# First DFT step of the filter in 64x64 tiles: leaving out the zero blocks of a block-diagonal factor

## The chip, the core and the metric

The kernel runs on one core of a Trainium2 chip. A core has a matrix engine (TensorE, PE in the profile; its weight loads stand apart as PEld), a vector engine (DVE), a scalar engine (ACT), a general engine (POOL) and a queue engine (SP) that here issues nearly all transfers. Sixteen DMA engines move the data. The metric is the device time of one execution in microseconds; runs are told by their median.

## The reference

An adaptive layer norm block with two branches, on 2048 tokens of 640 channels, all float32:

```
mod = silu(c) @ w_mod                        # six rows of 640: sa, ca, ga, sb, cb, gb
h   = layernorm(q) * (1 + ca) + sa
k_shift = causal depthwise conv of k, 4 taps
kv  = k_shift * v
y   = irfft(rfft(kv, 4096) * rfft(ssm_k, 4096))[:2048] + kv * ssm_D    # per channel
x   = q + ga * (h * y)
h   = layernorm(x) * (1 + cb) + sb
out = x + gb * (W2 gelu(W1 h + b1) + b2)     # mixer MLP across the 2048 tokens, F = 1728
```

The change touches the long convolution alone: the transform of `ssm_k` (one filter of length 2048 for each of the 640 channels).

## The kernel before

The 640 channels go through the convolution in five blocks of 128 (`c` = 0 to 4). The convolution is a transform of length 4096 with half of the input zero, written as matrix products on the matrix engine. A channel's 2048 values are a 64 by 32 array, and the transform has two steps with small DFT matrices: `step1` over the 64-long index, `f2` over the 32-long one, with the twiddle factors in the second matrix. Two inputs go through both steps: `kv`, called side 0, and the filter `ssm_k`, called side 1. After `f2` the two spectra are multiplied (`mul` on DVE, `add` mostly on POOL, both recorded at line 60 by a helper), and `i2` and `i1` turn the product back. `gate` multiplies the result into the normed `q` and adds it to the rows.

The partition axis of a `step1` operand is 2 x 64: two halves `h` of the 128 channels, each with the 64-long index. The DFT factor `F1` (128 rows) is therefore block-diagonal: for the real and for the imaginary part (`ri`) it has 128 columns, 64 for each half, and rows of one half are zero in the columns of the other. For a step `t` (four in each block), `step1(side, t)` takes 8 pieces `a`, and multiplies each with both parts: 16 products with 128 rows contracted, 64 stationary columns and 128 moving columns (line 229). `ri` decides which half of the output partitions is written. One ACT copy (line 231) then brings the result from PSUM into the tile `Z`, whose last axis pairs two channels. `f2(g)` reads `Z` at line 245 as moving operand: 64 columns, made of 32 pairs that lie 256 elements apart. All these operands are float32; in the profile one such product shows as two weight loads and two matmuls. `i1` at line 293 works in 64x64 tiles already: 64 rows contracted, 64 columns out, four positions of the array used in turn, and the two row halves write to different PSUM banks.

The order on every engine is written out by hand, with three PSUM slots of two banks used in turn. Ahead of the loop stand the four steps of side 0 and the four steps of side 1 for block 0. In the loop over `c`, `f2` runs eight times, then `i2`, then `i1(0)`, `i1(1)` and the gates. Side 1 of the next block comes at the end: for `c` = 1, 2, 3 `step1(1, 0)` stands between `i1(0)` and `i1(1)` (line 657) and the other three behind `i1(1)` (line 665); for `c` = 0 all four stand behind `i1(1)`. The DVE order there is: gate of half 0, three operations that prepare `kv` two blocks ahead (`dv`), gate of half 1, further `kv` operations, then `mul` of `f2(0)`. In the last block these are row statistics instead. The rest of the program, from about 300 us on, is the MLP (lines 443, 974 and 1051).

## Time and profile before

| | |
|---|---|
| median of 3 runs | 712.46 us (706.91 to 717.07) |
| span of the profiled execution | 705.8 us |
| time of PE, busy | 644.5 us |
| time of DVE, busy | 492.5 us |
| time of ACT, busy | 307.1 us |
| time of POOL, busy | 155.9 us |
| matmuls of line 229 on side 1 | 640, busy 39.6 us |
| matmuls of line 229 on side 0 | 640, busy 44.3 us |
| matmuls of line 245 (`f2`) | 2560, busy 95.8 us |

The profile's span is that of the recorded instructions. The profiled execution's own time isn't given beside it; the fastest run stands 1.1 us above the span, the median 6.7 us. A matmul's duration in the profile holds its way through the array, in which several matmuls are under way at once; how fast they follow each other is read from a stretch and its count. In a timeline a row is start, length, engine, line, operation, output and inputs, and the number of instructions merged in it; a bracket at its end gives the idle time before it and what ended that. "issue" there means that nothing the profile shows was waited for. Side 1 of `step1` is named `pst<-v,p`, side 0 `pst<-v,x`.

### The profile page before, as it was taken

The page shows a single profiled execution, that of the slowest core. Times are in us where ns is not written, and L with a number is a line of the kernel's source. Part 1 is how long each engine was busy: PE and PEld are TensorE (multiplying, and loading weights), DVE is VectorE, ACT ScalarE, POOL GpSimd, SP SyncE. Part 2 cuts the span into 40 slices and gives each one's busy share as a digit, 9 for nine tenths or more (in the row PEclk, how much of TensorE's full clock was granted, in tenths as well). Part 3 has the DMA queues.
Part 4 walks back from the last instruction along what each step waited for, and adds up shares of the span by engine and source line. Part 5 has one row for each costly group of instructions (what it writes and reads, how often), then busy time and mean ns, then how long its engine had stood idle before and what let it go on. Part 6 is the DMA issues. An engine that isn't in the chain of part 4 may idle for free.

```text
span 705.8 us, 20785 instructions
## 1 busy us (share of the span) xinstructions
PE 644.5 (91%) x9131; PEld 624.2 (88%) x9131; DVE 492.5 (70%) x861; ACT 307.1 (44%) x473; POOL 155.9 (22%) x135
## 2 busy tenths in 40 slices
PE   0699779989999989977899999999999999999997
PEld 0699469889999989777899999999999999999997
DVE  7778468969879638888884312311298979888886
ACT  0664554645745645556767223222334322333331
POOL 5297039615526428100010000000000000000000
PEclk9999979999999999999999999999999999999999
DMA  9968978446333522361303543354163243555511
GB/s 180 219 205 238 350 148 168 110 76 144 68 62 88 172 59 68 115 150 30 60 1 60 99 82 60 61 103 77 52 194 105 88 149 99 166 170 170 148 60 38
DMA packets 166672, 82.80 MB, mean 117 GB/s; under 512 B 89235, under 2 KB 157622, under 8 KB 166582
## 3 DMA queue, kind: packets, MB, share of 16 engines
q1 hardware_dynamic: 162034, 80.17, 46.0%
q10 hardware_dynamic: 4548, 1.31, 1.1%
q8 instruction: 71, 1.16, 0.7%
q14 instruction: 19, 0.16, 0.1%
HBM read 70.97 MB, written 10.49 MB: 115 GB/s over the span
## 4 chain that ended last, share of the span: by engine, by line
PE 65%; DVE 16%; ACT 4%; DMA 4%; POOL 4%; issue 3%; SPq 2%; ACTq 0%; DVEq 0%; POOLq 0%
PE pst L443 21%; PE pst L974 17%; PE pst L1051 7%; PE pst L229 7%; PE pst L245 6%; PE pst L274 4%; POOL y L60 3%; DVE tap L60 3%; PE pst L293 2%; DVE kt L60 2%; DVE p L60 2%; DMA aux<-in_w_mod_dram 2%; SPq L163 2%; DVE aux L60 1%; DVE y L60 1%
## 5 line engine op out<-in xcount | busy, mean ns | idle before, releaser
L245 PEld LDWEIGHTS pst<-z,w 128*64 128x64 f32 x2560 | 94.6, 141 | 7.9 <-ACT z L231 7.3
L245 PE MATMUL pst<-z,w 128*64 128x64 f32 x2560 | 95.8, 240 | 6.2 <-ACT z L231 6.1
L60 POOL TENSOR_TENSOR y<-p 128x256 f32<-128x256 f32 x72 | 92.3, 1341 | 22.4 <-DVE p L60 21.9
L60 DVE TENSOR_TENSOR p<-pst,kt 128x512 f32<-128x512 f32 x80 | 52.4, 691 | 23.8 <-ACT kt L249 15.5
L229 PE MATMUL pst<-v,x 128*64 128x128 f32 x640 | 44.3, 297 | 23.6 <-DVE x L60 23.6
L231 ACT ACTIVATE z<-pst 128x1024 f32<-128x1024 f32 x40 | 45.9, 1148 | 42.7 <-PE pst L229 23.1
L229 PEld LDWEIGHTS pst<-v,x 128*64 128x64 f32 x640 | 42.5, 220 | 24.1 <-POOL t L468 23.5
L847 ACT ACTIVATE pst<-pst,sm 128x640 f32<-128x640 f32 x14 | 10.7, 767 | 85.7 <-PE pst L443 85.7
L249 ACT ACTIVATE kt<-pst 128x512 f32<-128x512 f32 x40 | 25.1, 627 | 47.4 <-PE pst L245 26.6
L274 PEld LDWEIGHTS pst<-v,y 32*128 32x128 f32 x1280 | 38.1, 187 | 6.7 <-POOL y L60 3.8
L229 PE MATMUL pst<-v,p 128*64 128x128 f32 x640 | 39.6, 282 | 4.2 <-issue 2.2
L274 PE MATMUL pst<-v,y 32*128 32x64 f32 x1280 | 40.0, 272 | 3.8 <-DVE y L60 2.7
L974 PE MATMUL pst<-r_z,m_w 128*128 128x320 f32 x222 | 41.6, 309 | 0.7 <-DVE m_w L60 0.7
L229 PEld LDWEIGHTS pst<-v,p 128*64 128x64 f32 x640 | 36.9, 142 | 5.6 <-issue 2.9
L962 ACT ACTIVATE m_w<-m_v 128x896 fp32r<-128x896 f32 x24 | 22.2, 949 | 38.5 <-DVE m_v L60 23.1
L60 DVE TENSOR_TENSOR tap<-tap,kt 128x512 f32<-128x512 f32 x51 | 35.6, 698 | 1.3
L60 DVE TENSOR_TENSOR kt<-in,tap 128x512 f32<-128x512 f32 x51 | 35.0, 686 | 1.5
L974 PEld LDWEIGHTS pst<-r_z,m_w 128*128 128x128 f32 x222 | 34.8, 188 | 0.9 <-DVE m_w L60 0.9
L60 DVE TENSOR_TENSOR m_w<-m_v,m_w 128x896 fp32r<-128x896 f32 x24 | 26.0, 1088 | 9.5 <-ACT m_w L962 9.5
L282 ACT ACTIVATE z<-pst 128x512 f32<-128x512 f32 x38 | 21.5, 670 | 23.2 <-PE pst L274 23.2
L962 ACT ACTIVATE m_w<-m_p 128x896 fp32r<-128x896 f32 x12 | 11.5, 954 | 41.2 <-DVE m_p L60 24.4
L443 PE MATMUL pst<-r_z,wb0b 128*128 128x320 f32 x180 | 28.1, 310 | 0.9 <-DVE u_x L60 0.9
(278 smaller groups left out, 1436.9 us busy)
## 6 DMA issues: line engine op xcount, KB each, us to landing
x<-in_B_w_dram SPq DMA_DIRECT2D x22, 512.0 KB
m_v<-in_B_w_dram SPq DMA_DIRECT2D x15, 384.0 KB
x<-in_B_w_dram SPq DMA_DIRECT2D x14, 384.0 KB
aux<-in_A_ssm_k_dram SPq DMA_DIRECT2D x10, 512.0 KB
in<-in_A_k_dram SPq DMA_DIRECT2D x36, 128.0 KB
in<-in_A_v_dram SPq DMA_DIRECT2D x36, 128.0 KB
m_x<-xs SPq DMA_DIRECT2D x28, 160.0 KB
out_dram<-m_x SPq DMA_DIRECT2D x28, 160.0 KB
```

The source lines that it names most:

```text
L60: TT = lambda eng, o, a, b, op: eng.tensor_tensor(o, a, b, op=op)
L163: sync.dma_start(KSR[64 * h:64 * h + 64].rearrange("p (i n) -> p i n", i=64), dram(ssm_k, (DC * c + 64 * h) * S, [[32, 64], [S, 64], [1, 3 ...
L229: pe.matmul(ps[64 * ri:64 * ri + 64, o:o + 128], lhs, F1[:, 128 * ri:128 * ri + 128], start=True, stop=True)
L231: evac = lambda: act.activation(Z[:, side, t].rearrange("p a k e -> p e a k"), ps.rearrange("p (e a k) -> p e a k", a=8, e=2), AF.Copy)
L245: pe.matmul(ps[64 * h:64 * h + 64, o:o + 64], W2[k1 // 32][:, 2 * (k1 % 32) + ri], rhs, start=True, stop=True)
L249: act.activation(kt.rearrange("p (m i) -> p m i", i=32), pv[:, :, 1], AF.Copy)
L274: pe.matmul(pp[qd // 2][:, o:o + 64], Y[p, ri, i:i + 2].rearrange("p i k -> p (i k)"), V2[p, 64 * ri:64 * ri + 64], start=ri == 0, stop=ri ...
L282: act.activation(o, i, AF.Copy)
L443: pe.matmul(ps[0:m, h, 0:320], w_.bitcast(F32R), r_[:, 320 * h:320 * h + 320].bitcast(F32R), start=first and i == 0, stop=last and i == 2)
L962: act.activation(W[n][0].bitcast(F32R), A[p, w_], AF.Copy)
L974: pe.matmul(bank[n], w[:, i].bitcast(F32R), r.bitcast(F32R), start=i == 0 and k == 0, stop=i == 6 and k == 2)
L1051: pe.matmul(acc[s][:, h, 0:320], w[:, f_].bitcast(F32R), u[r + h].bitcast(F32R), start=f_ == 0 and k == 0, stop=f_ == NF - 1 and k == 2)
```

## The change

On side 1 each of the 16 products of a step becomes two: half `h` contracts its own 64 rows with its own 64 columns of `F1`, in a 64x64 tile, and writes to the PSUM bank of `h`. The blocks of zeros are not multiplied any more. A step has 32 products in place of 16, each with half the rows and half the moving columns. Side 0 keeps its 16 products, but puts their 128 output columns into two runs of 64, since the order of the pieces in PSUM and in `Z` is new for both sides: the half is the outer index, the piece the inner one. The ACT copy of side 1 reads PSUM with the pairing stride of 64 elements. `f2` reads its 32 pairs as eight groups, 1024 elements apart, of four pairs, 128 elements apart. The number of waits and of semaphore signals is the same on every engine.

```diff
         for a in range(8):
             i = 8 * t + a
             lhs = KSP[:, i] if side else X.rearrange("p (m i) -> p i m", i=32)[:, i]
-            o = 512 * (a % 2) + 128 * (a // 2)
             for ri in range(2):
-                pe.matmul(ps[64 * ri:64 * ri + 64, o:o + 128], lhs, F1[:, 128 * ri:128 * ri + 128], start=True,
-                          stop=True)
+                if not side:
+                    o = ps.rearrange("p (e h i k) -> p e i h k", e=2, h=2, i=4)[64 * ri:64 * ri + 64, a % 2, a // 2]
+                    pe.matmul(o, lhs, F1[:, 128 * ri:128 * ri + 128], start=True, stop=True)
+                    continue
+                for h in range(2):
+                    r, o = slice(64 * h, 64 * h + 64), 512 * h + 64 * a
+                    pe.matmul(ps[64 * ri:64 * ri + 64, o:o + 64], lhs[r], F1[r, 128 * ri + 64 * h:128 * ri + 64 * h + 64],
+                              start=True, stop=True)
         evac = lambda: act.activation(Z[:, side, t].rearrange("p a k e -> p e a k"),
-                                      ps.rearrange("p (e a k) -> p e a k", a=8, e=2), AF.Copy)
+                                      ps.rearrange("p (a e k) -> p e a k" if side else "p (e a k) -> p e a k", a=8, e=2),
+                                      AF.Copy)
         return evac if later else evac()
...
-                    rhs = bass.AP(tensor=T_z.tensor, offset=T_z.offset + 128 * h + 2 * k1,
-                                  ap=[T_z.ap[0], [256, 32], [1, 2]])
+                    rhs = bass.AP(tensor=T_z.tensor, offset=T_z.offset + 512 * h + 2 * k1,
+                                  ap=[T_z.ap[0], [1024, 8], [128, 4], [1, 2]])
```

## The prediction

> **What bounds the kernel now.** I read the page first: the span, the busy shares, the chain by line, and the groups of the operations that the change touches.

> ```profile
> span 705.8 us, 20785 instructions
> PE 644.5 (91%) x9131; PEld 624.2 (88%) x9131; DVE 492.5 (70%) x861; ACT 307.1 (44%) x473; POOL 155.9 (22%) x135
> ...
> q8 instruction: 71, 1.16, 0.7%
> ...
> L245 PE MATMUL pst<-z,w 128*64 128x64 f32 x2560 | 95.8, 240 | 6.2 <-ACT z L231 6.1
> ...
> L229 PE MATMUL pst<-v,p 128*64 128x128 f32 x640 | 39.6, 282 | 4.2 <-issue 2.2
> ```

> PE is busy 91% of the span, but an average: the question is what ends last where side 1 of `step1` stands. Two things count later. The 640 matmuls of side 1 occupy 39.6 us, which bounds the whole matter. And queue q8, which brings instructions, carried 71 packets of 1.16 MB / 71 = 16.3 KB, while PE has 9131 loads and as many matmuls: 18262 / 71 = 257, so about one packet for 256 PE instructions.

> Next the timeline of PE around side 1, for the turn from block 1 to 2 (`c` = 1), and behind it the chain that leaves there.

> ```profile
> 148.03 2.10 PE L293 MATMUL pst<-z,v 64*64 64x64 f32 x128
> 150.06 0.66 PE L229 MATMUL pst<-v,p 128*64 128x128 f32 x8
> 151.70 1.53 PE L229 MATMUL pst<-v,p 128*64 128x128 f32 x24 [0.98 <-issue]
> 153.16 1.75 PE L293 MATMUL pst<-z,v 64*64 64x64 f32 x104
> 155.70 0.58 PE L293 MATMUL pst<-z,v 64*64 64x64 f32 x24 [0.80 <-issue]
> 156.21 5.46 PE L229 MATMUL pst<-v,p 128*64 128x128 f32 x96
> ```

> ```profile
> 156.35 1.23 DVE aux L60
> ...
> 166.82 1.28 DVE p L60 x2
> ...
> 173.57 10.61 POOL y L60 x8
> ...
> 187.37 0.66 PE pst L274 x14
> ```

> The reader should see two things. First, the chain leaves PE when `i1(1)` ends at 156.3: the gate on DVE (156.35), thirteen `kv` operations, `mul` (166.82), POOL's additions, `i2` (187.37). The 5.46 us of `step1` behind 156.21 are not in it. Second, PE stops twice, for 0.98 and 0.80 us, with nothing to wait for, and between the two resumptions lie 24 + 104 = 128 matmuls with 128 loads: exactly 256 instructions. So PE waits for its own instructions. From one resumption to the next it took 155.70 - 151.70 = 4.00 us; while `i1` needs only 2.10 us for such a block (16.4 ns for a load with its matmul, "a pair" below) and side 1 now needs 5.46 / 96 = 56.9 ns a pair.

> The other turns, in the same two views:

> ```profile
> 202.01 1.96 PE L229 MATMUL pst<-v,p 128*64 128x128 f32 x30 [0.25 <-issue]
> ...
> 251.99 0.33 PE L293 MATMUL pst<-z,v 64*64 64x64 f32 x4 [0.70 <-issue]
> 252.25 1.97 PE L229 MATMUL pst<-v,p 128*64 128x128 f32 x32
> 254.15 2.37 PE L293 MATMUL pst<-z,v 64*64 64x64 f32 x128
> 256.44 5.46 PE L229 MATMUL pst<-v,p 128*64 128x128 f32 x96
> 263.13 3.11 PE L245 MATMUL pst<-z,w 128*64 128x64 f32 x78 [1.23 <-ACT z L231]
> ```

> ```profile
> 205.74 0.72 PE pst L293 x30
> ...
> 206.49 1.22 DVE aux L60
> ```

> For `c` = 2 the block takes 205.74 - 202.01 = 3.73 us, and the gate leaves PE in the same way. I take 3.87, the middle of 3.73 and 4.00, where the trace of before has no resumption of its own. Only for `c` = 3 does side 1 itself stand on the path: `f2` starts at 263.13, when the copy behind its last step is done.

> **The change part by part.** *Side 1.* A step has 32 pairs now (32 products of two) and 64 afterwards. The new product has the shape of line 293 (64x64, 64 columns, four tile positions), so I take 16.4 ns a pair: 64 x 16.4 = 1.05 us in place of 1.82. Over 20 steps that frees 15.4 us of PE. Each step also issues 64 instructions more. Four steps make 256, one whole block: so outside of these stretches every block boundary stays at the place in the work where it is now, and inside I can move them by counting.

> *c = 1.* Until 151.70 nothing differs. Then 56 pairs of the step remain (0.92 us, to 152.6) in place of 24; `i1(1)` starts, but the next boundary comes after 128 pairs, so 72 of its pairs run (1.18 us, to 153.8) and PE stands until 155.70, as it does now. Behind that boundary 56 pairs of `i1(1)` are left in place of 24. Its end moves by 32 x 16.4 = **+0.52 us**. The gate, thirteen DVE operations and `mul` are queued behind it, POOL behind them. Further on: 72 pairs of `step1`, a stand until 155.70 + 3.87 = 159.57, 120 pairs, to 161.5 or so, where the steps now end at 161.67. So `f2` gains 0.1 at most, then meets a boundary eight pairs in (163.4, 0.3 us); `mul` has to come at 167.34 by DVE, and this is covered.

> *c = 2.* The same with 205.74: **+0.52 us**.

> *c = 3.* `i1(0)` ends as now. The step takes 1.05 us (to 253.1), 60 pairs of `i1(1)` to 254.1, a stand until 251.99 + 3.87 = 255.86 (today the boundary lies at its pair 92, hence 2.37 in place of 2.10 us), 68 pairs to 257.0, 60 pairs of `step1` to 258.0, a stand until 259.73, and 132 pairs: 261.9, the end of before. With 3.73 it would be 261.6, with 4.00 262.2: **+0.15** for the path, from -0.3 to +0.4.

> *c = 0* and the start:

> ```profile
> 35.25 2.43 ACT L231 ACTIVATE z<-pst 128x1024 f32<-128x1024 f32 x2
> ...
> 40.02 1.09 ACT L231 ACTIVATE z<-pst 128x1024 f32<-128x1024 f32 x1 [0.59 <-PE pst L229]
> 40.84 11.65 SPq L512 DMA_DIRECT2D xa<-in_A_q_dram  x16
> 52.53 12.10 SPq L512 DMA_DIRECT2D xb<-in_A_q_dram  x16
> 64.67 1.12 SPq L346 DMA_DIRECT2D v<-in_w_mod_dram  x2
> 65.83 2.94 SPq L346 DMA_DIRECT2D aux<-in_w_mod_dram  x2
> ...
> 77.27 1.28 PE L353 MATMUL tap<-aux,sm 128*32 128x320 f32 x12 [1.15 <-DMA aux<-in_w_mod_dram]
> ...
> 99.52 4.23 POOL L60 TENSOR_TENSOR t<-in,t 128x512 f32<-128x512 f32 x2 [19.27 <-DMA in<-in_A_k_dram]
> ...
> 104.00 5.38 PE L229 MATMUL pst<-v,p 128*64 128x128 f32 x64 [1.96 <-DVE aux L60]
> ...
> 116.83 5.55 POOL L60 TENSOR_TENSOR y<-p 128x256 f32<-128x256 f32 x4
> ...
> 123.01 12.45 POOL L60 TENSOR_TENSOR y<-p 128x256 f32<-128x256 f32 x10
> ```

> At the start ACT follows with four copies of 1.2 us, two of them until 37.68; so `f2` may begin at about 40.1, some 1.0 us earlier. That gain is lost at 77.27, where PE waits for a transfer: SP has been issuing without a gap since 40.84, and no transfer there waits for `f2`. For `c` = 0 the third step waits for DVE until 104.00 either way; `f2` gains 1 to 3 us, but POOL works without a gap from 99.52 to 135.46, and its additions end that stage. Both count nothing. Without these covers they would bring 1 and up to 3.

> *The new operands.* Side 0's output in two runs, side 1's copy with another stride, and `f2`'s operand in groups of four pairs have no row of their own. For `f2` one bound is 2 x 16.4 = 32.8 ns a pair (half as many tiles as `i1`) against 95.8 / 2560 = 37.4 now: for `c` = 3 alone, where PE sets the pace, 512 x 4.6 ns = -2.4 us. The other bound is what a spread operand costs on side 0:

> ```profile
> 240.79 2.33 PE L229 MATMUL pst<-v,x 128*64 128x128 f32 x32
> ```

> 72.8 ns a pair against 56.9, 1.28 times. I take nothing: runs of two elements and 64 columns remain. The copy of ACT reads as many elements from as many banks; it is covered behind the stands of PE.

> The sum: 0.52 + 0.52 + 0.15 = **+1.2 us**, 0.2%: 707.0 us for the profiled span, 713.7 for the median, which lies 6.7 us above the span. About 2% is what a measurement of this kernel can tell from no change.

> [...]

> **The rivals.**

> *Blocks come in time.* If PE never stood for instructions, `i1(1)` would end at 150.13 + 1.05 + 2.1 = 153.3, and the gate would follow DVE's own queue:

> ```profile
> 152.79 0.70 DVE L60 TENSOR_TENSOR tap<-tap,kt 128x512 f32<-128x512 f32 x1
> ```

> at 153.5 in place of 156.35 (-2.85 us, twice). For `c` = 3 the four copies of ACT behind `i1(1)` would set `f2`: 251.3 + 1.05 + 2.1 + 4 x 1.2, about 259.2, -3.9. Together **-9.6**. All freed PE time would be -15.4. Against it stand the stops of today, with less to issue.

> *The clock falls* (slower). The granted clock:

> ```profile
> 97.00:104.00 7.00, 4.08 (x65) 3.59 (x64) 5.37 (x5) 4.39 (x8) 4.40 (x3) 1.00 0.73 164
> 104.00:108.50 4.50, 4.50 (x52) 4.50 (x54) 4.29 (x7) 1.12 (x1) 4.27 (x4) 0.62 0.77 160
> ...
> 148.00:156.00 8.00, 6.19 (x283) 5.57 (x286) 5.29 (x7) 1.19 (x1) 2.38 (x1) 1.00 0.57 102
> ```

> Behind a stretch with PE busy 4.08 of 7.00 us (58%) the clock was 0.62 over 4.5 us, that is half speed for some 3.4 us; behind 77% it stayed full. With the change PE works 2.1 us of every 3.87, 54%. If that cuts the clock, the 56 pairs behind 155.70 take 0.92 more, twice, and `f2` of `c` = 3 starts up to 1.7 later: **+4.7** in all. [...]

> *The tiles bring no better rate.* If two row halves don't run side by side, a pair takes 56.9 / 2 = 28.5 ns and a step what it takes today, so the change does not shorten it; the instructions double all the same. The gates still move by 0.52 twice, and for `c` = 3 the last 132 pairs take 3.8 us: **+2.7**. Against it: line 293 in the same tiles.

> *`f2` becomes dearer*, by 1.28 at most: 37.4 to 47.9 ns, 3.06 us for the 64 matmuls of a group in place of 2.39. For `c` = 1 and 2 POOL paces it at 10.61 / 4 = 2.65 us a group, so 8 x 0.41 = 3.3 each show; for `c` = 3 all of 8 x 0.67 = 5.3, and at the start some 3 beyond the transfers: **+15**.

> **How the numbers follow.** The forecast 0.55, the clock 0.20, blocks in time 0.10, tiles no faster 0.08, `f2` 0.07. Predicted 713.7. The range reaches down to the first rival, 712.46 - 9.6 = 703, cut to 704 as its whole size is unlikely, and up to the clock's 717.2 with most of the scatter of the runs shown (4.6) on it, 721. Faster by over 2% (14 us) would need nearly all freed PE time: 0.04. Slower by as much takes the full price of `f2`, or the clock with a slow `f2`: 0.08. Within 2%: 0.88.

> **What would show it.** q8 with 76 packets. Side 1 with 1280 matmuls at some 16 ns a pair between stops. Stops marked "issue" of 1.5 to 2 us inside `i1(1)` and inside the last three steps for `c` = 1, 2, 3, and resumptions 3.7 to 4.0 apart. The chain unchanged in its members, gates half a microsecond later. `f2`'s matmuls still busy 96 us. I am wrong if blocks follow each other faster than 3.7 us, if the clock row shows under 1.00 in these turns, or if those of `f2` take more.

## The result, and the profile after

The changed kernel takes 719.35 us (712.87 to 727.67), the kernel before in the same comparison 709.92 (703.62 to 723.14). The ratio is 1.0134, with a 95% interval of 1.0112 to 1.0156: about 9.5 us slower, where +1.2 was forecast. The time lies inside the range, but the forecast of nearly no change was wrong. The profiled execution has a span of 713.6 us, 7.8 more than before, and a time of 715.71.

From the page of the changed kernel: span, busy time, the clock in 40 slices, the instruction queue, and the groups of `f2` (line 251) and of side 1 (line 234). In a group's row stand count, busy time, mean of one in ns, and the idle time in front.

```profile
span 713.6 us, 22065 instructions
PE 633.4 (89%) x9771; PEld 614.6 (86%) x9771; DVE 493.4 (69%) x861; ACT 304.5 (43%) x473; POOL 157.2 (22%) x135
PEclk9999988999999799999999999999999999999999
q8 instruction: 76, 1.25, 0.7%
L251 PE MATMUL pst<-z,w 128*64 128x64 f32 x2560 | 100.1, 247 | 7.6 <-ACT z L236 6.2
...
L234 PE MATMUL pst<-v,p 64*64 64x64 f32 x1280 | 25.1, 229 | 17.8 <-issue 10.4
```

The clock's row of the page of before:

```profile
PEclk9999979999999999999999999999999999999999
```

PE is busy 11.1 us less (644.5 to 633.4) in a span that is 7.8 us longer. The five packets more on q8 are the 1280 added instructions, at 256 each. The clock is reduced in slices where it wasn't before: among them the fourteenth (232 to 250 us), where `i2` of the turn from block 3 to 4 runs. `f2` is busy 4.3 us more, with the same matmuls. Side 1 is busy 14.5 us less (39.6 to 25.1; 15.4 had been worked out), but the idle time in front of it that ended with "issue" grew from 2.2 to 10.4 us.

The timeline of PE of the changed kernel, turn `c` = 1:

```profile
147.20 2.10 PE L299 MATMUL pst<-z,v 64*64 64x64 f32 x128
149.12 0.29 PE L234 MATMUL pst<-v,p 64*64 64x64 f32 x8
150.63 1.04 PE L234 MATMUL pst<-v,p 64*64 64x64 f32 x56 [1.23 <-issue]
151.50 1.23 PE L299 MATMUL pst<-z,v 64*64 64x64 f32 x72
154.64 1.04 PE L299 MATMUL pst<-z,v 64*64 64x64 f32 x56 [1.91 <-issue]
155.50 1.11 PE L234 MATMUL pst<-v,p 64*64 64x64 f32 x64
157.02 0.34 PE L234 MATMUL pst<-v,p 64*64 64x64 f32 x8 [0.41 <-ACT z L236]
158.91 1.98 PE L234 MATMUL pst<-v,p 64*64 64x64 f32 x120 [1.55 <-issue]
162.21 0.51 PE L251 MATMUL pst<-z,w 128*64 128x64 f32 x8 [1.31 <-ACT z L236]
...
163.74 2.54 PE L251 MATMUL pst<-z,w 128*64 128x64 f32 x51 [1.03 <-issue]
```

Every count is the one that was worked out: 56 pairs of the step, 72 of `i1(1)`, a stand, 56, 72, a stand, 120, and eight of `f2` ahead of the last stand. What is larger than forecast is the time of a block: 150.63 to 154.64 is 4.01 us, then 4.27, then 4.83, in place of 3.87. The stand inside `f2` is 1.03 us long, not 0.3.

The same view for `c` = 3:

```profile
255.52 0.69 PE L299 MATMUL pst<-z,v 64*64 64x64 f32 x31
...
261.01 1.21 PE L299 MATMUL pst<-z,v 64*64 64x64 f32 x66 [1.54 <-issue]
...
264.47 2.09 PE L234 MATMUL pst<-v,p 64*64 64x64 f32 x128 [1.26 <-issue]
268.20 0.33 PE L234 MATMUL pst<-v,p 64*64 64x64 f32 x4 [1.63 <-issue]
269.75 20.23 PE L251 MATMUL pst<-z,w 128*64 128x64 f32 x512 [1.23 <-ACT z L236]
```

Here the periods are 3.46 and 3.73 us. The count differs from the forecast in one place: the sum let 132 pairs run behind its last boundary, but a block ends after 128, and the trace shows 128, a stand of 1.63 us, and the last four. From the start of `i1(0)` to `f2` it takes 14.2 us (269.75 - 255.52) against 13.9 before (263.13 - 249.20): +0.3, near the forecast of +0.15. So the lag was there already. All three turns, from `i1(0)` to `f2`, take 15.0, 13.0 and 14.2 us against 14.9, 13.8 and 13.9 before, 42.2 in place of 42.6 together, at a granted clock of 1.00. In this execution the stands of the turns thus cost no more than those of before.

Behind the turn `c` = 2 `f2` starts 0.4 us later than before (213.47, 213.06), behind the turn `c` = 3 it starts 6.6 later (269.75, 263.13). The time between is seen in the windows: PE, its loads, DVE, ACT and POOL busy with their counts, the granted clock, DMA's share and GB/s. First before, then the changed kernel.

```profile
236.00:240.00 4.00, 3.29 (x109) 3.06 (x109) 4.00 (x9) 3.07 (x2) 0.68 (x1) 1.00 0.02 4
240.00:251.00 11.00, 11.00 (x344) 10.62 (x342) 3.58 (x5) 6.85 (x10) 0.00 (x0) 1.00 0.44 98
```

```profile
236.00:240.00 4.00, 2.19 (x52) 1.92 (x52) 4.00 (x9) 2.06 (x3) 2.03 (x2) 0.99 0.07 26
240.00:251.00 11.00, 11.00 (x188) 10.55 (x187) 5.43 (x7) 4.43 (x6) 0.00 (x0) 0.54 0.44 98
```

From 240 to 251 PE works without a gap in both, but at a clock of 0.54 it gets through 188 matmuls in place of 344. In front of it lie 1.81 us in which PE had nothing to do, in place of 0.71. The timeline shows what it was, and what it cost `i2` (before, then after):

```profile
237.29 3.58 PE L274 MATMUL pst<-v,y 32*128 32x64 f32 x120 [0.71 <-DVE y L60]
```

```profile
238.63 6.52 PE L280 MATMUL pst<-v,y 32*128 32x64 f32 x128 [1.75 <-DVE y L60]
245.08 3.69 PE L230 MATMUL pst<-v,x 128*64 128x128 f32 x32
```

`i2(0)` waits 1.75 us for the sums of `y`, then runs at half speed (a granted clock of 0.50 from 240 to 245 us); the step of side 0 behind it takes 3.69 us in place of 2.33. From the start of these products to that of `i1(0)` the lag grows by some 5 us. The `f2` behind the turn `c` = 3 adds another 1.2, in part at half speed (0.66 from 270 to 275, 1.00 before). Behind the turn `c` = 1 the first `mul` comes 1.3 us later, counted from `i1(0)`; in front of it lie both the stand of 1.03 us inside `f2` and half speed from 164.8 to 168.2 (0.51), and how they share it is not shown. So in this execution some 6 to 7 of the 7.8 us pass at a lower clock. Over all runs the mean clock of the changed kernel is 0.964, that of the kernel before 0.980.

### The profile page after: what moved, and what is told of

Its sections match the earlier page's. It is cut to its first block, busy times and chain, and to the rows that moved or that the text cites. A ratio compares the mean times of both kernels' runs of the same rounds, so it can differ in the third digit from the quotient of the medians.

```text
span 713.6 us, 22065 instructions
## 1 busy us (share of the span) xinstructions
PE 633.4 (89%) x9771; PEld 614.6 (86%) x9771; DVE 493.4 (69%) x861; ACT 304.5 (43%) x473; POOL 157.2 (22%) x135
## 4 chain that ended last, share of the span: by engine, by line
PE 68%; DVE 14%; ACT 6%; issue 4%; POOL 4%; SPq 2%; DMA 1%; ACTq 0%; DVEq 0%
PE pst L449 21%; PE pst L980 17%; PE pst L251 9%; PE pst L1057 7%; PE pst L280 5%; PE pst L230 4%; POOL y L60 3%; PE pst L299 2%; DVE tap L60 2%; PE pst L234 2%; ACT z L236 2%; DVE kt L60 2%; DVE aux L60 1%; SPq L163 1%; DVE p L60 1%
## 5 line engine op out<-in xcount | busy, mean ns | idle before, releaser
L251 PE MATMUL pst<-z,w 128*64 128x64 f32 x2560 | 100.1, 247 | 7.6 <-ACT z L236 6.2
L251 PEld LDWEIGHTS pst<-z,w 128*64 128x64 f32 x2560 | 98.8, 149 | 8.9 <-ACT z L236 7.0
L60 POOL TENSOR_TENSOR y<-p 128x256 f32<-128x256 f32 x72 | 93.9, 1347 | 29.8 <-DVE p L60 29.4
L60 DVE TENSOR_TENSOR p<-pst,kt 128x512 f32<-128x512 f32 x80 | 52.3, 690 | 28.6 <-ACT kt L255 21.0
L230 PE MATMUL pst<-v,x 128*64 128x128 f32 x640 | 46.7, 308 | 23.5 <-DVE x L60 23.5
L230 PEld LDWEIGHTS pst<-v,x 128*64 128x64 f32 x640 | 44.6, 222 | 24.1 <-POOL t L474 23.5
L236 ACT ACTIVATE z<-pst 128x1024 f32<-128x1024 f32 x40 | 44.3, 1135 | 46.7 <-PE pst L299 18.9
L280 PEld LDWEIGHTS pst<-v,y 32*128 32x128 f32 x1280 | 40.9, 200 | 6.8 <-POOL y L60 3.6
L280 PE MATMUL pst<-v,y 32*128 32x64 f32 x1280 | 42.9, 286 | 3.6 <-DVE y L60 2.5
L234 PE MATMUL pst<-v,p 64*64 64x64 f32 x1280 | 25.1, 229 | 17.8 <-issue 10.4
L234 PEld LDWEIGHTS pst<-v,p 64*64 64x64 f32 x1280 | 22.6, 143 | 19.7 <-issue 11.5
L60 DVE TENSOR_TENSOR tap<-tap,kt 128x512 f32<-128x512 f32 x51 | 35.5, 697 | 1.3
L60 DVE TENSOR_TENSOR kt<-in,tap 128x512 f32<-128x512 f32 x51 | 35.0, 687 | 1.5
L60 DVE TENSOR_TENSOR m_w<-m_v,m_w 128x896 fp32r<-128x896 f32 x24 | 26.0, 1088 | 9.6 <-ACT m_w L968 9.6
L299 PEld LDWEIGHTS pst<-z,v 64*64 64x64 f32 x1280 | 21.4, 139 | 9.6 <-issue 6.8
L299 PE MATMUL pst<-z,v 64*64 64x64 f32 x1280 | 23.1, 224 | 7.0 <-issue 5.8
```

Source lines behind the costliest of these rows:

```text
L60: TT = lambda eng, o, a, b, op: eng.tensor_tensor(o, a, b, op=op)
L230: pe.matmul(o, lhs, F1[:, 128 * ri:128 * ri + 128], start=True, stop=True)
L234: pe.matmul(ps[64 * ri:64 * ri + 64, o:o + 64], lhs[r], F1[r, 128 * ri + 64 * h:128 * ri + 64 * h + 64], start=True, stop=True)
L236: evac = lambda: act.activation(Z[:, side, t].rearrange("p a k e -> p e a k"), ps.rearrange("p (a e k) -> p e a k" if side else "p (e a k) ...
L251: pe.matmul(ps[64 * h:64 * h + 64, o:o + 64], W2[k1 // 32][:, 2 * (k1 % 32) + ri], rhs, start=True, stop=True)
L280: pe.matmul(pp[qd // 2][:, o:o + 64], Y[p, ri, i:i + 2].rearrange("p i k -> p (i k)"), V2[p, 64 * ri:64 * ri + 64], start=ri == 0, stop=ri ...
```

## The experiments

All ratios are to the kernel before, with 95% intervals.

**The new places alone.** Side 1 keeps its 16 products and the old stride of its ACT copy. The new order in PSUM and in `Z` and the new operand of `f2` stay:

```diff
-                if not side:
+                if True:
...
-                                      ps.rearrange("p (a e k) -> p e a k" if side else "p (e a k) -> p e a k", a=8, e=2),
+                                      ps.rearrange("p (e a k) -> p e a k", a=8, e=2),
```

> The new order of pieces alone: side 1 keeps its 16 products with the zero blocks, but both sides write PSUM and Z in the new order and f2 reads groups of four pairs. Theory (more instructions make PE stand between blocks, and the stands lower the clock of what follows): as before, ratio 0.998 to 1.002, q8 71 packets. Rival (the new operand of f2 or the copy's stride costs the time): 1.013 like the change, and f2's matmuls busy over 98 us without more time at half clock.

0.9993 (0.9961 to 1.0025). The operands' new order costs nothing that can be measured, `f2`'s in eight groups of four pairs among them, so that rival is not in the 1.3%. The new stride of side 1's copies was not tested here; the profiles show 44.3 us for the 40 copies of `step1` after the change and 45.9 before, so they did not become longer.

**The added instructions without the tiles.** Every product is split in two, but contracts all 128 rows:

```diff
-                    r, o = slice(64 * h, 64 * h + 64), 512 * h + 64 * a
-                    pe.matmul(ps[64 * ri:64 * ri + 64, o:o + 64], lhs[r], F1[r, 128 * ri + 64 * h:128 * ri + 64 * h + 64],
+                    o = 512 * h + 64 * a
+                    pe.matmul(ps[64 * ri:64 * ri + 64, o:o + 64], lhs, F1[:, 128 * ri + 64 * h:128 * ri + 64 * h + 64],
```

> The change's number of instructions without its tiles: each of the 16 products of a side 1 step becomes two with all 128 rows and 64 columns, zeros included. I take f2's 37 ns a pair, 2.4 us a step. Theory: 128 pairs last 4.8 us and no longer wait for the next block, so PE hardly stands inside the steps; the gates of c = 1 and 2 are half a microsecond late and f2 starts some 2 later, +4.9 us, ratio 1.005 to 1.008, mean clock as before (0.98). Rival (the number of instructions costs by itself, however fast they run): 1.013. Rival (64x64 tiles lower the clock, not the stands): 1.005 to 1.008 too, so this run doesn't tell that from the theory.

1.0085 (1.0050 to 1.0121): 6.0 us for twice as many products, at a mean clock of 0.978. Its timeline for `c` = 1:

```profile
150.39 2.10 PE L299 MATMUL pst<-z,v 64*64 64x64 f32 x128
...
153.89 1.90 PE L234 MATMUL pst<-v,p 128*64 128x64 f32 x56 [1.01 <-issue]
155.72 1.28 PE L299 MATMUL pst<-z,v 64*64 64x64 f32 x72
158.44 1.05 PE L299 MATMUL pst<-z,v 64*64 64x64 f32 x56 [1.44 <-issue]
159.41 2.37 PE L234 MATMUL pst<-v,p 128*64 128x64 f32 x72
162.71 3.77 PE L234 MATMUL pst<-v,p 128*64 128x64 f32 x120 [0.94 <-issue]
167.72 4.51 PE L251 MATMUL pst<-z,w 128*64 128x64 f32 x116 [1.24 <-ACT z L236]
```

The counts are those of the changed kernel (56, 72, 56, 72, 120), the periods 4.55 and 4.27 us. From `i1(0)` to `f2` it takes 17.3 us, against 14.9 before. For `c` = 2 and 3 it is 15.0 and 15.3 against 13.8 and 13.9. That is 5 us in three turns, and not at a lower clock by the durations: `i1(0)` takes 2.10 us for 128 matmuls in the first two and 2.08 for 124 in the third, as before at 1.00. Only about half of it are stands: those marked "issue" add up to 5.4 us, against 2.7 before. The other half are longer steps: a pair takes 31 to 35 ns here and 38 in one step (2.46 us for 64), so two take 63 to 77 where one of the old took 56.9, and the twelve steps take 25.5 us in place of 22.9. It had been expected that PE would hardly stand inside these steps, and that does not hold. The changed kernel is 0.49% slower still (give or take 0.42, from the two intervals), 3.5 us, with the same instructions, less work in the array, and a clock of 0.964.

**Tiles with as many instructions as before.** The operands of side 1 are bfloat16 (`FB` holds the blocks of `F1` in this type), so that a product is one load and one matmul (the trace shows 32 matmuls for a step's 32 products):

```diff
-    KSP = P.rearrange("p (i m) -> p i m", i=32)
+    KSP = P.bitcast(BF)[:, 0:2048].rearrange("p (i m) -> p i m", i=32)
...
-                    pe.matmul(ps[64 * ri:64 * ri + 64, o:o + 64], lhs[r], F1[r, 128 * ri + 64 * h:128 * ri + 64 * h + 64],
+                    pe.matmul(ps[64 * ri:64 * ri + 64, o:o + 64], lhs[r], FB[r, 64 * ri:64 * ri + 64],
```

> The change's tiles with before's number of instructions: the two operands of side 1 are rounded to bf16, so a product is one load and one matmul, 64 instructions a step. (The filter's transform is computed in lower precision.) Theory: the stops are those of before, i1(1) ends at the same time in each turn, f2 starts 1 to 2 us earlier for c = 3; PE waits longer for ACT's copies ahead of f2, so the clock may still fall there. Ratio 0.997 to 1.005. Rival (small tiles lower the clock by themselves): 1.010 to 1.015.

1.0031 (0.9994 to 1.0068), as expected: with 64 instructions a step most of the loss is gone, and nothing is won. The clock is 0.941, the lowest of all kernels here. Its timeline for the turn `c` = 2:

```profile
187.78 5.03 PE L282 MATMUL pst<-v,y 32*128 32x64 f32 x120 [0.97 <-DVE y L61]
...
202.52 2.10 PE L301 MATMUL pst<-z,v 64*64 64x64 f32 x128
...
213.01 1.23 PE L253 MATMUL pst<-z,w 128*64 128x64 f32 x18 [1.82 <-ACT z L238]
```

From `i1(0)` to `f2` the three turns take 12.7, 10.5 and 10.0 us, 9.4 less than before together. But the 120 matmuls of `i2` take 5.03 us in place of 3.58, in part at half speed, and from the start of `i2` to `i1(0)` the three rounds take 15.3, 16.2 and 16.3 us in place of 13.4, 13.2 and 13.1, 8.0 more together. So the time that hardly moves is the sum of a gain and a loss of about the same size, and the lower clock has its price here too.

**Fewer instructions.** First the array's work as before with a quarter of the instructions, 512 columns a product:

```diff
+            if side and a > 1:
+                break
...
+                f = F1[:, 128 * ri:128 * ri + 128]
+                if side:
+                    o = 512 * a
+                    pe.matmul(ps[64 * ri:64 * ri + 64, o:o + 512].rearrange("p (b k) -> p b k", b=4), lhs,
+                              f[:, None, :].to_broadcast([128, 4, 128]), start=True, stop=True)
```

> Before's array work with a quarter of its instructions: a side 1 step is four products with 512 moving columns, each taking one piece of the filter for four (the filter's transform isn't computed; the time on the array is the same). Theory: 48 instructions less a step, 960 in all, q8 67 or 68 packets; in each turn one stop of 0.8 to 1 us less, gates of c = 1 and 2 up to 1 us earlier: ratio 0.994 to 0.999, clock at least that of before. Rival (instructions don't matter): 0.999 to 1.002 with the stops where they were.

0.9960 (0.9930 to 0.9991) with 68 packets on q8, both as expected; the clock of 0.975 is a little below that of before, which was not. Then the tiles of the change with an eighth of its instructions:

```diff
+            if side and a:
+                break
...
-                    pe.matmul(ps[64 * ri:64 * ri + 64, o:o + 64], lhs[r], F1[r, 128 * ri + 64 * h:128 * ri + 64 * h + 64],
-                              start=True, stop=True)
+                    f = F1[r, 128 * ri + 64 * h:128 * ri + 64 * h + 64]
+                    pe.matmul(ps[64 * ri:64 * ri + 64, 512 * h:512 * h + 512].rearrange("p (b k) -> p b k", b=8), lhs[r],
+                              f[:, None, :].to_broadcast([64, 8, 64]), start=True, stop=True)
```

> The change's tiles with an eighth of its instructions: a side 1 step is four products in 64x64 tiles with 512 moving columns, each taking one piece of the filter for all eight (the filter's transform isn't computed). The array works some 0.9 us a step, as in the change, but PE doesn't stand for instructions there. Theory that idle PE of any cause lowers the clock: PE now waits for ACT's copies instead, clock 0.955 to 0.970, ratio 0.994 to 1.006. Theory that only the stands between blocks do it: clock 0.976 to 0.982, ratio 0.986 to 0.993.

0.9899 (0.9874 to 0.9923) at a clock of 0.972: the time is that of the second theory, the clock lies between the two. In its timeline for `c` = 1 the stands are gone, but for 0.20 us:

```profile
147.65 2.10 PE L302 MATMUL pst<-z,v 64*64 64x64 f32 x128
149.57 1.04 PE L237 MATMUL pst<-v,p 64*64 64x512 f32 x8
150.43 1.11 PE L302 MATMUL pst<-z,v 64*64 64x64 f32 x64
151.73 1.16 PE L302 MATMUL pst<-z,v 64*64 64x64 f32 x64 [0.20 <-issue]
152.72 1.04 PE L237 MATMUL pst<-v,p 64*64 64x512 f32 x8
```

Eight pairs of 512 columns take 1.04 us, where 64 pairs of 64 columns take 1.11 in the changed kernel: the array time is nearly the same. `i1(1)` ends at 152.9, 5.2 us behind the start of `i1(0)`, where it took 8.3 before and 8.5 after the change. The time differs by 2.35% between these two, 16.6 us, and it comes with the number of instructions: a step has 16 in place of 128, at nearly the same array time. Against the kernel before, the tiles with this few instructions bring 7.2 us: the prediction's first rival, worked out at 9.6.

The same with the old tile shape, half of the products left out:

```diff
+            if side and a:
+                break
...
+                if side:
+                    pe.matmul(ps[64 * ri:64 * ri + 64, 0:512].rearrange("p (b k) -> p b k", b=4), lhs,
+                              f[:, None, :].to_broadcast([128, 4, 128]), start=True, stop=True)
```

> The same array time a step as the one in 64x64 tiles with 512 columns, without these tiles: two products with all 128 rows and 512 columns, one piece for four, and the copy reads that half of PSUM twice (half of the filter's products are left out, and the rest isn't its transform). Theory that idle PE lowers the clock, whatever the tile: clock and ratio within 0.004 of the kernel with the tiles. Rival (a 64x64 tile uses less of the array, and that lowers the clock): clock 0.976 or more here, ratio 0.986 to 0.993, and the kernel with tiles lower in clock.

0.9914 (0.9886 to 0.9942), at a clock of 0.972, as with the wide tiles (0.972). So, within these intervals, neither the time nor the clock hangs on the tiles' shape.

**Where the loss sits.** The tiles for blocks 0 and 1 alone, whose steps stand ahead of the loop and at `c` = 0, and for blocks 2, 3 and 4 alone (`block >= 2`), the turns `c` = 1, 2, 3:

```diff
+        block = count[side] // 4
+        count[side] += 1
+        whole = not side or not (block < 2)
...
-                if not side:
+                if whole:
```

> Tiles for channel blocks 0 and 1 only (the start and the turn c = 0), where transfers and POOL end last; the other blocks keep the zero blocks, in the new order of pieces. Theory: PE stands for instructions there too, but what it loses is absorbed at the transfers and by POOL: ratio 0.998 to 1.004. Rival (stands and low clock cost wherever they are): half of the change's 1.3%, 1.005 to 1.008.

1.0022 (0.9989 to 1.0054), as expected, with an interval that just reaches the rival's (from 1.005). But its profile does not show stands that are absorbed: the `f2` behind `c` = 0 starts 4.4 us earlier than before (106.22, 110.58), and the turns behind it, whose products are the old ones, give that back and more, with three stretches of 6.8 us at half speed (from 135, 190 and 241 us). Before has none there.

> Tiles for channel blocks 2, 3 and 4 only (the turns c = 1, 2, 3). Theory: all of the change's cost is here, 1.010 to 1.015, clock 0.960 to 0.972. Rival: 1.005 to 1.008.

1.0103 (1.0060 to 1.0147). Nearly all of the loss comes with the tiles of the three turns, as in the sum, though the clock is 0.975, above what was expected; the two parts add up to the whole (0.22 + 1.03 against 1.34%).

**Spare work against the low clock.** Three spare products of 256 columns ahead of `f2(0)` and of `i2(0)`, first with the change, then without:

```diff
+        if g == 0:
+            warm(ps, T_w2[0])
...
+        if c:
+            warm(pp[0], T_v1)
```

> The changed kernel with 27 spare products of 256 columns (0.43 us each) on the matrix engine where it waits for others: three ahead of f2(0) in each block, while ACT still copies side 1, and three ahead of i2(0) for c = 1 to 4, while POOL still adds. Their results are overwritten. Theory (the change costs through the clock, which falls behind stretches in which PE is idle): mean clock from 0.964 back to 0.972 or more, ratio to before 1.000 to 1.008. Rival (the stands between instruction blocks are the cost themselves, and the clock is chance): the spare work adds instructions and at best changes nothing, 1.012 to 1.018.

1.0115 (1.0079 to 1.0150), a miss: the clock rises to 0.975, the time hardly falls.

> The kernel before with the same 27 spare products. Theory: its clock is 0.979 already, so there is less to win: clock 0.983 or more, ratio 0.994 to 1.000. Rival: 1.000 to 1.004.

1.0008 (0.9979 to 1.0038), a small miss as well. The pair tells more than each alone. PE of the changed kernel with spare products, `c` = 2, then of the kernel before with them:

```profile
201.66 2.10 PE L307 MATMUL pst<-z,v 64*64 64x64 f32 x128
...
206.30 1.56 PE L307 MATMUL pst<-z,v 64*64 64x64 f32 x91 [1.05 <-issue]
...
209.76 2.09 PE L234 MATMUL pst<-v,p 64*64 64x64 f32 x128 [1.32 <-issue]
213.76 0.69 PE L234 MATMUL pst<-v,p 64*64 64x64 f32 x29 [1.91 <-issue]
214.37 1.56 PE L243 MATMUL pst<-w 128*128 128x256 f32 x6
215.87 1.34 PE L257 MATMUL pst<-z,w 128*64 128x64 f32 x30
```

```profile
199.34 2.10 PE L301 MATMUL pst<-z,v 64*64 64x64 f32 x128
201.36 1.97 PE L229 MATMUL pst<-v,p 128*64 128x128 f32 x32
203.26 2.10 PE L301 MATMUL pst<-z,v 64*64 64x64 f32 x128
205.29 5.46 PE L229 MATMUL pst<-v,p 128*64 128x128 f32 x96
210.68 1.56 PE L237 MATMUL pst<-w 128*128 128x256 f32 x6
212.17 5.03 PE L251 MATMUL pst<-z,w 128*64 128x64 f32 x131
```

Three spare products take 1.50 us here (214.37 to 215.87), 0.50 each, where 0.43 had been taken. With the old products PE does not stand at all here, and with the new ones it stands three times; from `i1(0)` to `f2` it takes 14.2 us (215.87 - 201.66) against 12.8. Over the three turns, from the start of `f2` for `c` = 1 to that for `c` = 4 (line numbers aside, the same work), it is 157.5 against 152.8 us, and each of the two has one half-speed stretch of 3.4 us in it. So 4.7 us there come from stands and not from the clock. This holds against a kernel that does not stand at all: from `i1(0)` to `f2` the three turns take 44.3 and 38.9 us in this pair, and 42.2 and 42.6 without spare products, where the kernel before stands too.

**Another order.** `step1(1, 0)` behind `i1(1)`, so that the gate has less ahead of it, with the change and then without:

```diff
-            elif c:
-                k0 = step1(1, 0, True)
-            elif half:
+            elif half and not c:
...
-        if c:
-            k0()
-        for t in range(1 if c else 0, 4):
+        for t in range(4):
```

> The changed kernel with the first step of side 1 moved from between i1(0) and i1(1) to behind i1(1). By the count of instructions i1(1) then ends near 153.8 in place of 155.7 for c = 1 and the gate some 2 us earlier, while the four steps still stand for two blocks and f2 starts when it does in the change. If the late gate is the cost, the ratio falls to 1.000 to 1.006; if it is the start of f2 and the clock behind the stands, it stays at 1.008 to 1.014.

1.0084 (1.0051 to 1.0117): in the reading with `f2` and the clock (1.008 to 1.014), with an interval that just reaches into that of the gate (to 1.006).

> The same order with before's products: i1(0) and i1(1) follow each other and the gate comes some 2 us earlier; f2's start hardly moves, so mul(0) waits for f2 instead of DVE and comes about 1 us earlier for c = 1 and 2: ratio 0.995 to 0.999.

1.0049 (1.0015 to 1.0083), a miss: an earlier gate is not a gain even without the change, since `f2` then starts later (15.6, 14.1 and 14.9 us behind `i1(0)`, against 14.9, 13.8 and 13.9). The order does not separate the theories well; it rather speaks against the gate as the place of the loss.

**Spare work inside the stands.** One spare product in front of `i1(1)` and of each of the last three steps, where PE would stand anyway, with the change and without:

```diff
+        if side and t:
+            spare(ps, 512 if t == 2 else 256)
...
+        if half:
+            spare(ps, 512)
```

> The changed kernel, with one spare product in front of i1(1) and of each of the three last steps of side 1 in the turns c = 1, 2, 3 (128 rows contracted, 512 or 256 columns, written to a bank that the step then overwrites), 9 to 16 instructions more per turn. The spare product fills the array in time in which PE would stand for its instructions anyway, and about none of it is on the path. If the lower clock is most of the cost, the clock rises from 0.964 to 0.974 or more and the time goes to 1.003-1.008 of the kernel before. If the stands themselves, or a later gate, are the cost, it stays at 1.010-1.016 even where the clock rises.

1.0118 (1.0086 to 1.0151) at a clock of 0.971. The clock rises less than was asked of it (0.974) and the time stays, which was named as the branch of the stands.

> The kernel before with the same spare products at the same places. PE has its blocks busier there already, so the clock should hardly change (0.980 to 0.985) and the spare products have less stand to hide in: 0.999-1.006. Below 0.997 would say that the kernel before, too, loses time to a clock that falls in these stretches.

1.0149 (1.0113 to 1.0184), a miss by far: here the spare products lie on the path. So the same spare work costs 10.6 us on the kernel before and nothing that can be measured on the changed one, though it is issued there as well. The stands do not take it in: in the profile of the changed kernel with spare products the three turns take 47.1 us from `i1(0)` to `f2`, in place of 42.2, while the rest of the three rounds takes 110.2 in place of 117.8, without any half speed between 115 and 300 us. In these executions it is the clock that pays for the spare work.

## Why the prediction was wrong

**The counting was right, but for one boundary.** A product of two loads and two matmuls, blocks of 256, boundaries moved by counting pairs: the counts came out for `c` = 1 and 2, and q8 carried the 76 packets. For `c` = 3 the sum missed the boundary four pairs ahead of the end of the steps, which cost a stand of 1.63 us. The 1280 matmuls run at 16 to 19 ns a pair between stands (1.98 us for 120, 1.04 for 56).

**The gates.** +0.52 each was forecast. From the start of `i1(0)` to the end of `i1(1)` the profile shows 8.5 us in place of 8.3 for `c` = 1, and 7.0 in place of 7.1 for `c` = 2. For the start of `f2` at `c` = 3, +0.15 was forecast and +0.3 came. The forecast terms are no larger than that in this execution. The last one came near by luck: its own working gives 261.9, which is the end of before, and so 0 with a range of -0.3 to +0.25; and the stand that it missed was made up for by a first boundary that came 5.5 us behind the start of `i1(0)` (261.01 - 255.52), where 6.7 had been worked out (255.86 - 249.20).

**One step that failed: one period for all blocks.** The sum took 3.87 us for every block. The runs show 3.46 to 4.83 within one execution, and turns without any stand where spare products stood ahead of them. The cover of `f2`'s start behind `c` = 1 ("a boundary eight pairs in, 0.3 us") failed with it, since that boundary cost 1.03. In the profiled execution of the change the three turns together did not become longer by this (42.2 us, 42.6 before). Splitting the products, with as many instructions as the change, cost 6.0 us (3.5 to 8.6) at an almost unchanged clock, in place of 1.2; about half of what its three turns show are stands, the rest longer products.

**The step that cost most: the clock as a rival and not as a term.** The prediction gave the clock a chance of 0.20, a price of 4.7 us, and the three turns of side 1 as its place. In the sum it stood at nothing. It happened, but behind the turns: the granted clock is 1.00 in all three of them, with PE busy for 57, 68 and 60% of the time from `i1(0)` to `f2`. Behind the first and the third it is 0.51 (164.8 to 168.2) and 0.50 (271 to 274). The largest part lay where no step of the change is, in `i2` for `c` = 3, 25 us behind the turn `c` = 2 and behind a wait of 1.75 us for DVE. The 4.00 us ahead of it show PE idle for 1.81.

The profile of one execution puts some 6 to 7 of 7.8 us on slow stretches. Over many runs an estimate comes from those at the same mean clock, 0.971 to 0.976: the kernel before takes 711.3 us (mean of 23 runs), the changed kernel 714.1 (mean of 4). So about 3 of the 9.5 us are there at an equal clock, and the rest goes with the lower clock. How they divide exactly stays open, since a mean clock does not tell where in the program it fell. What sets off each slow stretch stays open as well: with tiles for blocks 0 and 1 alone it came in turns whose products are the old ones. What is shown is that the number of instructions decides: the same tiles with nearly the same array time take 16.6 us less with an eighth of them.

**The start.** -1.0 was forecast and covered by transfers. The timeline shows the opposite sign:

```profile
37.11 0.69 PE L234 MATMUL pst<-v,p 64*64 64x64 f32 x31 [0.41 <-ACT z L236]
40.63 0.73 PE L234 MATMUL pst<-v,p 64*64 64x64 f32 x33 [2.84 <-issue]
42.54 19.99 PE L251 MATMUL pst<-z,w 128*64 128x64 f32 x512 [1.17 <-ACT z L236]
```

PE stands 2.84 us for a block, and `f2` starts at 42.54 in place of 41.16. No stand for a block had been assumed there. The cover held: behind `c` = 0 `f2` starts 0.8 us earlier than before (109.80, 110.58). The experiment with blocks 0 and 1 alone gives 1.0022 with an interval that holds 1.

**`f2`.** Its new operand costs nothing, as taken (0.9993). Its matmuls are busy 95.7 us with the new places alone and with the split products, as before (95.8), so the 4.3 us more of the change are not the operand; `f2` runs in part at half speed there (0.51 from 164.8 to 168.2, 0.50 from 271 to 274). The sign that was named for a dearer operand would have been read wrongly without that experiment.

**The rivals.** Blocks in time has the right mechanism and nearly the size where the instructions are few: 7.2 us measured, 9.6 worked out, and behind `i1(0)` the end of `i1(1)` for `c` = 1 comes 3.0 us earlier (2.85 worked out), `f2` for `c` = 3 3.8 earlier (3.9). But this kernel doubles the instructions and cannot have it. "Tiles no faster" is out: 1.11 us for the 64 pairs of a step. A dearer `f2` is out.

## What to carry to other kernels

Count the instructions of the matrix engine beside its array time: where a stretch already stands for its instructions, a product split into smaller tiles trades array time, which was free there, for instructions, which were not: here PE is busy 14.5 us less on side 1, and the kernel takes 9.5 us more. A float32 product counts four here (320 products more on side 1 brought 1280 instructions); the same tiles gave 0.990 with 512 moving columns and 1.013 with 64. When such a change empties the array, ask also where PE waits next: here the largest part of the lower clock, 0.54 from 240 to 251 us, lay there and not in the changed lines. And read a time that does not move by its stretches: it can be a gain and a loss.

## What the runs showed of the hardware

Where PE stood for its instructions in the loop, a block of 256 took 3.46 to 4.83 us to follow the one before. In the changed kernel it was 4.01, 4.27 and 4.83 us in the turn `c` = 1, with the DMA engines busy for 0.85 of the time, and 3.46 to 4.00 in the two others, with 0.32 and 0.42; whether the one is the cause of the other was not tested. At the start, behind 7.8 us with the DMA engines busy for 0.96 of the time, a single stand was 2.84 us. One stand is not like the next: the kernel before stands for 0.98 and 0.80 us in the turn `c` = 1, and with the spare products ahead of `f2(0)` and `i2(0)` it does not stand in that turn.

A mean clock alone does not give the time. The kernel with bfloat16 tiles ran at 0.941 and 1.0031, since what it lost at the lower clock it had won in the turns; the kernel with spare products in the stands of before ran at 0.983 and 1.0149.
